# Attention scores on eight array tiles, attention sums on four, in pairs of PSUM banks, ahead of a gated feed-forward layer

## The chip, the cores and the metric

The kernel runs on one core of one Trainium2 chip. The metric is the device time of one execution in microseconds (us). A core has five engines that run side by side and meet only at semaphores: TensorE (PE, matrix products; its loads of stationary operands are listed apart as PEld), VectorE (DVE), ScalarE (ACT), GpSimd (POOL) and SyncE (SP, which issues the DMAs here). TensorE writes to PSUM, which has eight banks of 512 fp32 values in each of 128 partitions.

## The reference

The inputs are q, k, v of shape (4, 8, 768, 64), eight memory keys and values for each head, and the weights of the second layer.

```python
for c in range(24):                                  # chunks of 32 queries
    k_ctx = k[:, :, max(0, 32*c - 16) : min(768, 32*c + 40)]
    k_full = concatenate([mem_k, k_ctx], axis=2)     # up to 64 keys, v_full alike
    s = matmul(q_c, k_full.T) / 8
    a = exp(s - max(s)); a = a / (sum(a) + 1e-9)
    out[:, :, 32*c : 32*c + 32] = matmul(a, v_full)
x = heads put side by side                           # (4, 768, 512)
h = maximum(x @ w_in, 0)                             # (4, 768, 1024)
conv = 3-tap convolution of h along the sequence, a tap triple for each channel
result = (h / (1 + exp(-conv))) @ w_out              # (4, 768, 512)
```

The weights reach the chip as 64-bit floats. The kernel decodes each into a high and a low part.

## The kernel before, in words

**Attention.** There are 32 steps (`attention(n)`): four batches, two halves of the sequence, four pairs of heads. A step holds 12 chunks of two heads, that is 24 products of 32 queries by 64 keys. The host lays q, k and v out for it (`_laid_out`).

- *Scores* (L375 to L389). 24 fp32 matmuls, each with a stationary operand of 64 rows (the head's 64 dimensions) by 32 queries and 64 moving columns (keys). A row half of the array belongs to a head, and of the eight 64x32 tiles that the array has, four are used: head 0 writes to partition blocks 0 and 2, head 1 to blocks 1 and 3. TensorE runs an fp32 matmul as two passes, each with its own load of the stationary operand, so the trace has 48 matmul and 48 load records for a step. The scores fill 384 columns of one bank (pool `s`, two banks).
- *Softmax* (L391 to L439). DVE takes the maxima (L393); then DVE subtracts and ACT takes one exponential (L398, L404), or ACT takes six with a bias (L419). DVE sums (L431) and inverts (L433), and DVE or POOL multiplies (L436).
- *Turn* (L443 to L484). In a step of kind P, TensorE transposes three 128x128 blocks into a bank (L448), and ACT copies the result with two instructions (L455) into `a_d`. That tile is as wide as two row halves with zeros in half of it, so that a product over all 128 rows picks one chunk's keys for each half of the columns. In a step of kind B, DVE transposes 32x32 blocks (L466), and three DMAs take the result through DRAM. The string `TURN` names each step's kind: 15 P and 17 B.
- *Sums* (L486 to L497, `values`). 12 fp32 matmuls on two 128x64 tiles: 128 rows (two chunks of 64 keys), 64 columns of stationary v, 64 moving columns of `a_d`, so 24 passes. ACT (L498) and DVE (L501) take the result from its bank into a high and a low part. Turned blocks and sums share the pool `ta`, two banks.

**Feed-forward.** `ffn_in` is 768 matmuls of 384 columns (L517), with a ReLU on ACT; `gated` is the convolution, a tanh and products on DVE, ACT and POOL; `ffn_out` is 552 matmuls of 512 columns and 48 of 256 (L579). They use the other four banks (pool `f`).

**Order.** The list `ORDER` fixes the order in which all 1,545 operations are issued, and so the order on every engine. TensorE works strictly in it: between stretches of feed-forward matmuls stand short excursions to scores and sums. Strings of letters (`TAP`, `MULT`, `LO`, `SOFT`, `NORM`, `CLEAR`) choose the engine of an operation for each step or block. The costs in `plan.op` are not executed. A tile takes a free slot of its pool when its first operation is issued and gives it back after its last.

Of the kernel before, what the change touches and what calls it, by code (L numbers as in the profile page):

```python
# [22 lines left out]
KC = STEP * (NC - 1) + KW  # L23
# [6 lines left out]
W_IN, W_OUT, W_CONV = "RCMSMMCC", "MmCMCCmM", "r"  # L30
TAP = "AAAVAAAAVAAAAAAAVAAAVVAVVVVVVVAA"
MULT = "VVGVGGGGGVVVGVVVVVVVGVGVVVVVGVVG"
LO = "VVVGVVVVGVVGVGVGVVVGVVGGVVGVGGGG"
SOFT = "VVVVCCACVVCAVVVCVACACCCCCACCCCVV"
NORM = "VVGGGVGGGGVVVGGGVVGGGVGVGVVGGVVG"
CLEAR = "GAGAVAAGAGGVVAVAVVGAGGVGAAVVAVGV"
KEEP = "KKKNNNNKNKNKKNNKKKKNKNNNKKNNNKKN"
HOME = "wwwwwwwwwwxwwwwwxwwwwwwwxxwxxwxw"
TURN = "PPPPPPPPBPPBBPBPBPBBBBPBBBBPBBBB"

NU, NK, NE, NA, N64, ND = 40, 3, 3, 2, 4, 4

ORDER = [
# [154 lines left out]
def attention_then_gated_ffn(  # L198
# [35 lines left out]
    for x in slots("a_d", NA, [P, 2, 4 * NG, CH]):  # L234
        G.memset(x, 0.0)
# [127 lines left out]
    def attention(n):  # L363
# [79 lines left out]
        if TURN[n] == "P":  # L443
            t = Tile("ta")

            def turn():
                for g in range(NG):
                    nc.tensor.transpose(out=t.t[:, g * P : (g + 1) * P], in_=e.t[:, g, 1 : 2 * KW + 1], identity=ident)  # L448
# [255 lines left out]
```

## Time and profile before

| | |
|---|---|
| median of three runs | 350.18 us (350.15 to 351.26) |
| the profiled execution's own time | 349.44 us |
| its span (first to last instruction) | 347.7 us |
| TensorE busy | 333.2 us, 96% of the span |
| loads of stationary operands | 297.8 us, 86% |
| DVE, ACT, POOL busy | 244.3, 202.7, 86.0 us |
| bytes moved by DMA | 49.10 MB, 141 GB/s |

Busy time is the union of an engine's records. Ends of matmul records are modelled and the records overlap, so for TensorE the starts say more than the durations. In tables of windows, (x4) is the number of records that touch the window.

### The profile page before, as it was taken

To read this page: it belongs to the slowest core of one execution; us is meant where nothing else is said; L and a number is where in the kernel's file an instruction comes from. 1 tells how busy PE (TensorE), PEld (TensorE's weight loads), DVE (VectorE), ACT (ScalarE), POOL (GpSimd) and SP (SyncE) were. 2 spreads that over 40 slices of the span, in tenths; PEclk is the share of its full clock that TensorE was granted. 3 is DMA by queue.
4 is the path that set the end of the run, shared out by engine and by line. 5 is a ranking of instruction groups with operands and counts; after the bars stand their busy time and mean duration, and the time that the engine had idled before them with its cause. 6 is when DMAs were issued, how large, how long until landed. Compare 5 with 4: busy or idle time off the path is not lost.

```text
span 347.7 us, 8950 instructions
## 1 busy us (share of the span) xinstructions
PE 333.2 (96%) x3717; PEld 297.8 (86%) x3717; DVE 244.3 (70%) x406; ACT 202.7 (58%) x447; POOL 86.0 (25%) x83
## 2 busy tenths in 40 slices
PE   1599999999999999999999999999999999999996
PEld 1488999999999999899888889899998888888886
DVE  3999999999989999889999659611285698220000
ACT  3488969899888899366786385322426633320111
POOL 3324121165524103220002462020002395020000
PEclk9999999999999999999999999999999999999999
DMA  7998877757777435602244533311000001110202
GB/s 270 399 304 267 290 274 237 233 176 220 247 223 254 147 119 169 205 20 83 90 139 146 180 116 116 128 47 43 20 0 32 31 30 48 61 74 0 92 35 86
DMA packets 27256, 49.10 MB, mean 141 GB/s; under 512 B 3152, under 2 KB 18128, under 8 KB 27216
## 3 DMA queue, kind: packets, MB, share of 16 engines
q1 hardware_dynamic: 27216, 48.53, 42.1%
q8 instruction: 29, 0.48, 0.5%
q14 instruction: 11, 0.09, 0.1%
HBM read 38.89 MB, written 9.63 MB: 140 GB/s over the span
## 4 chain that ended last, share of the span: by engine, by line
PE 92%; DMA 3%; DVE 3%; ACT 1%; SPq 0%; POOL 0%; issue 0%; ACTq 0%
PE f L579 39%; PE f L517 38%; PE ta L495 8%; PE s L384 6%; DMA w<-in_w_in_dram 2%; PE ta L448 2%; DMA w<-in_v_dram 1%; DVE e L436 0%; DVE w_top L287 0%; SPq L262 0%; POOL w_out_lo L344 0%; DVE e L398 0%; DVE z L431 0%; DVE top L393 0%; DVE w_top L294 0%
## 5 line engine op out<-in xcount | busy, mean ns | idle before, releaser
L517 PE MATMUL f<-u,w_in_hi 128*128 128x384 f32 x512 | 141.8, 343 | 0.0
L579 PE MATMUL f<-w_out_hi,u 128*128 128x512 f32 (+1 forms) x400 | 125.9, 387 | 0.0
L517 PEld LDWEIGHTS f<-u,w_in_hi 128*128 128x128 f32 x512 | 93.5, 188 | 2.1
L579 PEld LDWEIGHTS f<-w_out_hi,u 128*128 128x128 f32 x400 | 74.1, 188 | 15.6
L517 PE MATMUL f<-u,w_in_lo 128*128 128x384 f32 x256 | 86.4, 337 | 0.0
L547 DVE SCALAR_TENSOR_TENSOR u<-u,cw,u 128x767 f32<-128x767 f32 x64 | 70.9, 1121 | 10.6 <-ACT u L538 9.5
L579 PE MATMUL f<-w_out_lo,u 128*128 128x512 f32 (+1 forms) x200 | 77.2, 386 | 0.0
L517 PEld LDWEIGHTS f<-u,w_in_lo 128*128 128x128 f32 x256 | 48.1, 188 | 0.8
L590 ACT COPY w_top<-f 128x512 f32<-128x512 f32 (+1 forms) x25 | 14.1, 569 | 54.9 <-PE f L579 47.3
L527 ACT ACTIVATE u<-f 128x384 f32<-128x384 f32 x64 | 30.4, 492 | 25.1 <-PE f L517 25.0
L579 PEld LDWEIGHTS f<-w_out_lo,u 128*128 128x128 f32 x200 | 37.6, 188 | 7.2
L567 POOL TENSOR_TENSOR u<-u,u 128x768 fp32r<-128x768 f32 x13 | 25.9, 2006 | 67.6 <-ACT u L564 46.3
L436 POOL TENSOR_TENSOR e<-e,z 128x384 f32<-128x384 f32 x18 | 15.6, 866 | 79.4 <-DVE z L433 60.1
L564 ACT CAST u<-u 128x768 fp32r<-128x768 f32 x32 | 26.1, 835 | 11.9 <-PE f L579 6.6
L551 ACT ACTIVATE u<-u 128x768 f32<-128x768 f32 x32 | 26.7, 846 | 8.9 <-DVE u L547 8.9
L561 POOL TENSOR_TENSOR u<-u,u 128x768 f32<-128x768 f32 x11 | 23.2, 2117 | 28.4 <-ACT u L560 28.4
L567 DVE TENSOR_TENSOR u<-u,u 128x768 fp32r<-128x768 f32 x19 | 21.8, 1160 | 10.8 <-ACT u L564 4.7
L501 DVE TENSOR_TENSOR u<-ta,u 128x384 fp32r<-128x384 f32 x32 | 17.1, 541 | 16.7 <-ACT u L498 16.3
L556 DVE SCALAR_TENSOR_TENSOR u<-u,u 128x768 f32<-128x768 f32 x21 | 21.7, 1034 | 9.9 <-ACT u L551 9.9
L419 ACT ACTIVATE e<-s,top 128x64 f32<-128x64 f32 x120 | 26.6, 327 | 3.2 <-DVE top L411 2.1
L498 ACT CAST u<-ta 128x384 fp32r<-128x384 f32 x32 | 15.0, 479 | 14.4 <-PE ta L495 14.3
L384 PE MATMUL s<-k,u 64*32 64x64 f32 x1344 | 23.4, 219 | 0.0
(59 smaller groups left out, 336.9 us busy)
## 6 DMA issues: line engine op xcount, KB each, us to landing
u<-in_v_dram SPq DMA_DIRECT2D x25, 384.0 KB, 5.0
k<-in_k_dram SPq DMA_DIRECT2D x28, 252.0 KB, 3.7
u<-in_q_dram SPq DMA_DIRECT2D x32, 192.0 KB, 4.1
out_dram<-w_top SPq DMA_DIRECT2D x23, 256.0 KB, 2.0
w<-in_w_in_dram SPq DMA_DIRECT2D x8, 512.0 KB, 5.5
w<-in_w_out_dram SPq DMA_DIRECT2D x8, 512.0 KB, 4.6
t_dram<-w SPq DMA_DIRECT2D x17, 192.0 KB, 2.3
a_d<-t_dram SPq DMA_DIRECT2D x34, 96.0 KB, 3.1
```

What stands on the lines that cost most here:

```text
L384: nc.tensor.matmul(s.t[j * D + h * CH : j * D + (h + 1) * CH, o : o + KW], lhsT=q_[r, c], rhs=k_t.t[r, c * STEP : c * STEP + KW], start=Tr ...
L419: A.activation(keys(e)[:, g // 2, g % 2], s_()[:, g // 2, g % 2], AF.Exp, bias=top.t[:, g : g + 1], scale=SCALE)
L495: nc.tensor.matmul(y, lhsT=v_g[:, g, u, h], rhs=a_d.t[:, :, o], start=True, stop=True)
L517: nc.tensor.matmul(f.t[:, :TW], lhsT=w_in_p[c][:, fc, cc], rhs=x.t[:, a * TW : (a + 1) * TW], start=(cc == 0 and i == 0), stop=(cc == NCC ...
L527: "A", act(TW, True), lambda: A.activation(h.t[:, hf * TW : (hf + 1) * TW], f.t[:, :TW], AF.Relu, scale=0.5), (f,), ((h, hf),)
L547: lambda j=j, to=to, at=at: V.scalar_tensor_tensor(out=c.t[:, to], in0=h.t[:, at], scalar=w[j], in1=c.t[:, to], op0=ALU.mult, op1=ALU.add) ...
L551: plan.op("A", act(S), lambda: A.activation(c.t, c.t, AF.Tanh), (c,), (c,), table="exp")
L556: lambda: V.scalar_tensor_tensor(out=y.t, in0=c.t, scalar=1.0, in1=h.t, op0=ALU.add, op1=ALU.mult),
L561: plan.op("G", 2.42 * S, lambda: G.tensor_tensor(out=y.t, in0=c.t, in1=h.t, op=ALU.mult), (c, h), (y,), shared=True)
L564: plan.op("A", act(S), lambda: A.copy(out=g_hi.t, in_=y.t), (y,), (g[0],))
L567: lambda: (V if lo == "V" else G).tensor_tensor(out=g_lo.t, in0=y.t, in1=g_hi.t.bitcast(F32), op=ALU.subtract),
L579: nc.tensor.matmul(ps.t[:, :n], lhsT=gs[b, fc][a].t[:, tt * P : (tt + 1) * P], rhs=w_out_p[c][:, fc, o : o + n], start=(fc == 0 and i == 0 ...
```

## The change

Half of a step's chunks now belong to each row half of the array. The row half u holds the six chunks of half u, for both heads, and the results of the two row halves go to two different banks of a pair. The scores use all eight 64x32 tiles: 24 matmuls of the same shape as before. The sums are 24 matmuls on four 64x64 tiles instead of 12 on two 128x64 tiles: 64 rows (one chunk's keys), 64 columns of stationary v, and 32 moving columns. `a_d` holds no zeros: it is half as wide, its memsets go, and in steps of kind P one ACT copy fills it. Scores, turned blocks and sums share one pool of two slots, each a pair of banks, where there were two pools of two banks; `a_d` has three slots instead of two. The DMAs of kind B move the same bytes in runs of half the length. The host's layouts follow; the keys of a step are 528 columns wide instead of 504.

The order list and the strings of letters are new: 1,528 operations, 21 steps of kind P and 11 of kind B.

```diff
-W_IN, W_OUT, W_CONV = "RCMSMMCC", "MmCMCCmM", "r"
-TAP = "AAAVAAAAVAAAAAAAVAAAVVAVVVVVVVAA"
-MULT = "VVGVGGGGGVVVGVVVVVVVGVGVVVVVGVVG"
-LO = "VVVGVVVVGVVGVGVGVVVGVVGGVVGVGGGG"
-SOFT = "VVVVCCACVVCAVVVCVACACCCCCACCCCVV"
-NORM = "VVGGGVGGGGVVVGGGVVGGGVGVGVVGGVVG"
-TURN = "PPPPPPPPBPPBBPBPBPBBBBPBBBBPBBBB"
+W_IN, W_OUT, W_CONV = "CCCmmCCM", "MCCCCCmM", "r"
+TAP = "AAAVAAAAVAAAAVAAAAAAVVVAAAAAVVAV"
+MULT = "VGGVGGGGGVVGGGVVGGGVGGVVGVVGVVGV"
+LO = "GVVVVVVVGVVVGGVVGVGVVVVGGVGGGVVV"
+SOFT = "ACVVVCCVVVCCVVVCCCVCVVCCCVACVAVC"
+NORM = "GVGGGGGGVGGGVGGVGGGGVVVVVVVGGGGG"
+TURN = "PPPPPPPPBPPPPPBPBPPPPPPPBBBBBBBB"
...
-    for x in slots("a_d", NA, [P, 2, 4 * NG, CH]):
-        G.memset(x, 0.0)
+    slots("a_d", NA, [P, TW])
...
-    slots("s", 2, [P, 512], pool=psum)
-    slots("ta", 2, [P, 512], pool=psum)
+    slots("s", 2, [P, 2, 512], pool=psum)
...
-                for p in range(2):
-                    for j in range(2):
-                        c = 4 * g + 2 * j + p
-                        o = (2 * g + p) * KW
-                        for h in range(2):
-                            r = slice(h * D, (h + 1) * D)
-                            nc.tensor.matmul(
-                                s.t[j * D + h * CH : j * D + (h + 1) * CH, o : o + KW],
-                                lhsT=q_[r, c], rhs=k_t.t[r, c * STEP : c * STEP + KW], start=True, stop=True,
-                            )
+                for j in range(4):
+                    c, h = 2 * g + j // 2, j % 2
+                    o = h * KH + c * STEP
+                    for u in range(2):
+                        r = slice(u * D, (u + 1) * D)
+                        nc.tensor.matmul(
+                            s.t[j * CH : (j + 1) * CH, u, g * KW : (g + 1) * KW],
+                            lhsT=q_[r, c, h], rhs=k_t.t[r, o : o + KW], start=True, stop=True,
+                        )
...
-            for p in range(2):
-                r = slice(p * D, (p + 1) * D)
-
-                def place(r=r, p=p):
-                    A.copy(
-                        out=a_d.t[r, p].rearrange("p (r g) q -> p g r q", g=NG),
-                        in_=t.t[r, : NG * P].rearrange("p (g r q) -> p g r q", r=4, q=CH),
-                    )
+            plan.op("A", act(TW, True), lambda: A.copy(out=a_d.t, in_=t.t[:, 0, :TW]), (t,), (a_d,))
...
-            v_g = v_().rearrange("p (g c h d) -> p g c h d", g=NG, c=2, h=2)
-            for g in range(NG):
-                for u in range(2):
-                    for h in range(2):
-                        r = slice(h * D, (h + 1) * D)
-                        if TURN[n] == "P":
-                            o, y = (2 * u + h) * NG + g, a.t[r, g * P + u * D : g * P + (u + 1) * D]
-                        else:
-                            o, y = h * 6 + 2 * g + u, a.t[r, g * P : (g + 1) * P].rearrange("p (j u q) -> p u j q", j=2, u=2)[:, u]
-                        nc.tensor.matmul(y, lhsT=v_g[:, g, u, h], rhs=a_d.t[:, :, o], start=True, stop=True)
+            v_c = v_().rearrange("p (c h d) -> p c h d", c=HC, h=2)
+            for c in range(HC):
+                g, p = c // 2, c % 2
+                for h in range(2):
+                    j = 2 * p + h
+                    o = (4 * g + j) * CH if TURN[n] == "P" else (NG * j + g) * CH
+                    for u in range(2):
+                        r = slice(u * D, (u + 1) * D)
+                        nc.tensor.matmul(
+                            a.t[h * D : (h + 1) * D, u, c * CH : (c + 1) * CH],
+                            lhsT=v_c[r, c, h], rhs=a_d.t[r, o : o + CH], start=True, stop=True,
+                        )
```

## Rows read from the trace of the kernel before

**Rows 1.** The page: busy time, share of the span and instructions of each engine.
```profile
PE 333.2 (96%) x3717; PEld 297.8 (86%) x3717; DVE 244.3 (70%) x406; ACT 202.7 (58%) x447; POOL 86.0 (25%) x83
```
**Rows 2.** The page: the chain that ended last, by engine.
```profile
PE 92%; DMA 3%; DVE 3%; ACT 1%; SPq 0%; POOL 0%; issue 0%; ACTq 0%
```
**Rows 3.** Windows of 20 us: length, busy us and records by engine, clock, DMA share, GB/s.
```profile
20.00:40.00 20.00, 20.00 (x392) 18.30 (x388) 19.80 (x46) 17.65 (x54) 4.39 (x5) 1.00 0.87 291
40.00:60.00 20.00, 20.00 (x331) 19.33 (x328) 19.04 (x44) 15.98 (x43) 5.54 (x10) 1.00 0.73 238
...
140.00:160.00 20.00, 20.00 (x274) 18.24 (x273) 16.81 (x27) 11.34 (x22) 4.47 (x4) 1.00 0.39 119
...
300.00:320.00 20.00, 20.00 (x87) 16.09 (x87) 2.87 (x2) 4.08 (x6) 1.85 (x1) 1.00 0.10 39
```
**Rows 4.** Waits of TensorE over the whole span: us in total, times, longest us.
```profile
PE s L384 <- DMA u<-in_q_dram: 5.7, 1, 5.7
PE ta L448 <- DVE e L436: 2.6, 2, 2.0
...
PE ta L495 <- DMA w<-in_v_dram: 0.3, 1, 0.3
```
**Rows 5.** Timeline of TensorE, two excursions: start us, us, operation, records.
```profile
173.41 0.40 PE L579 MATMUL f<-w_out_hi,u 128*128 128x512 f32 x1
173.74 1.54 PE L384 MATMUL s<-k,u 64*32 64x64 f32 x96
...
175.55 0.39 PE L579 MATMUL f<-w_out_lo,u 128*128 128x512 f32 x1
...
202.05 0.40 PE L579 MATMUL f<-w_out_hi,u 128*128 128x512 f32 x1
...
206.29 0.34 PE L517 MATMUL f<-u,w_in_lo 128*128 128x384 f32 x1
206.47 0.33 PE L517 MATMUL f<-u,w_in_hi 128*128 128x384 f32 x1
```
**Rows 6.** Windows of line L384 alone, from an excursion's first scores: matmuls, then loads.
```profile
39.87:39.88 0.01, 0.01 (x2) 0.01 (x2) 1.00 0.41 154
...
39.87:39.90 0.03, 0.03 (x4) 0.03 (x5) 1.00 0.80 307
...
39.87:39.98 0.11, 0.11 (x8) 0.11 (x12) 1.00 0.52 196
39.87:41.10 1.23, 1.23 (x88) 1.23 (x92) 1.00 0.24 86
```
**Rows 7.** Windows of line L495 alone, from an excursion's first sums.
```profile
38.32:38.37 0.05, 0.05 (x2) 0.05 (x2) 1.00 1.21 489
38.32:38.39 0.07, 0.07 (x2) 0.07 (x4) 1.00 1.47 466
38.32:38.44 0.12, 0.12 (x4) 0.12 (x6) 1.00 1.12 373
38.32:39.60 1.28, 1.28 (x43) 1.28 (x45) 1.00 0.98 374
```
**Rows 8.** Windows of line L517 alone, from the first matmul after an excursion.
```profile
29.04:29.15 0.11, 0.10 (x1) 0.10 (x1) 1.00 0.90 330
29.04:29.16 0.12, 0.11 (x1) 0.12 (x2) 1.00 0.83 302
```
**Rows 9.** Timeline of TensorE, one turn inside a stretch of feed-forward.
```profile
25.11 0.49 PE L448 MATMUL ta<-ident,e 128*128 128x128 f32 x3
...
25.61 0.34 PE L517 MATMUL f<-u,w_in_lo 128*128 128x384 f32 x1
```
**Rows 10.** Groups of instructions: records, busy us, mean ns of one, idle before.
```profile
L556 DVE SCALAR_TENSOR_TENSOR u<-u,u 128x768 f32<-128x768 f32 x21 | 21.7, 1034 | 9.9 <-ACT u L551 9.9
...
L501 DVE TENSOR_TENSOR u<-ta,u 128x384 fp32r<-128x384 f32 x32 | 17.1, 541 | 16.7 <-ACT u L498 16.3
L498 ACT CAST u<-ta 128x384 fp32r<-128x384 f32 x32 | 15.0, 479 | 14.4 <-PE ta L495 14.3
```

More of the change, by code (lines that the diff above doesn't have):

```diff
@@ L22 @@
 NG = NC // 4
-KC = STEP * (NC - 1) + KW
+HC = NC // 2
+KH = STEP * (HC - 1) + KW
+KC = 2 * KH
 TINY = 1.75 * 2.0**-15
 WC = 512
-W_IN, W_OUT, W_CONV = "RCMSMMCC", "MmCMCCmM", "r"
-TAP = "AAAVAAAAVAAAAAAAVAAAVVAVVVVVVVAA"
-MULT = "VVGVGGGGGVVVGVVVVVVVGVGVVVVVGVVG"
-LO = "VVVGVVVVGVVGVGVGVVVGVVGGVVGVGGGG"
-SOFT = "VVVVCCACVVCAVVVCVACACCCCCACCCCVV"
-NORM = "VVGGGVGGGGVVVGGGVVGGGVGVGVVGGVVG"
-CLEAR = "GAGAVAAGAGGVVAVAVVGAGGVGAAVVAVGV"
-KEEP = "KKKNNNNKNKNKKNNKKKKNKNNNKKNNNKKN"
-HOME = "wwwwwwwwwwxwwwwwxwwwwwwwxxwxxwxw"
-TURN = "PPPPPPPPBPPBBPBPBPBBBBPBBBBPBBBB"
-NU, NK, NE, NA, N64, ND = 40, 3, 3, 2, 4, 4
-ORDER = [
[69 rows of a table removed]
+W_IN, W_OUT, W_CONV = "CCCmmCCM", "MCCCCCmM", "r"
[4 more added lines that the diff above has]
+NORM = "GVGGGGGGVGGGVGGVGGGGVVVVVVVGGGGG"
+CLEAR = "VVGGAGGAGGAGVVAAVAAGGAAAGAVVAGVG"
+KEEP = "KKNKKKKNKNKKNKKNNKKNKKNNKNKKKNKK"
+HOME = "wwwwwwwwxwxwwwwwwwwxwxwwwxxxwwxw"
+TURN = "PPPPPPPPBPPPPPBPBPPPPPPPBBBBBBBB"
+NU, NK, NE, NA, N64, ND = 40, 3, 3, 3, 4, 4
+ORDER = [
[68 rows of a table added]
 ]
@@ L247, in attention_then_gated_ffn @@
     slots("z", 4, [P, 2 * NG])
-    slots("s", 2, [P, 512], pool=psum)
-    slots("ta", 2, [P, 512], pool=psum)
+    slots("s", 2, [P, 2, 512], pool=psum)
     slots("f", 4, [P, 512], pool=psum)
-    slots("t_dram", ND, [2, 2, CH, 2, NG * KW], pool=dram)
+    slots("t_dram", ND, [2, 4, CH, 2, NG * CH], pool=dram)
     w_in_p = [const.tile([P, NFC, NCC, P], F32R, name=f"w_in_{p}") for p in ("hi", "lo")]
@@ L375, in scores @@
         def scores():
-            q_ = q_d.t[:, :TW].rearrange("p (c q) -> p c q", q=CH)
+            q_ = q_d.t[:, :TW].rearrange("p (c h q) -> p c h q", c=HC, h=2)
             for g in range(NG):
-                for p in range(2):
-                    for j in range(2):
-                        c = 4 * g + 2 * j + p
-                        o = (2 * g + p) * KW
-                        for h in range(2):
-                            r = slice(h * D, (h + 1) * D)
-                            nc.tensor.matmul(
-                                s.t[j * D + h * CH : j * D + (h + 1) * CH, o : o + KW],
-                                lhsT=q_[r, c], rhs=k_t.t[r, c * STEP : c * STEP + KW], start=True, stop=True,
-                            )
-        plan.op("PE", 700, scores, (q_d, k_t), (s,), mode="tiled", late=250)
-        s_ = lambda: s.t[:, :W].rearrange("p (g u k) -> p g u k", u=2, k=KW)
+                for j in range(4):
[7 more added lines that the diff above has]
+                        )
+        plan.op("PE", 365, scores, (q_d, k_t), (s,), mode="t32", late=250)
+        s_ = lambda: s.t[:, :, : NG * KW].rearrange("p u (g k) -> p g u k", k=KW)
         plan.op(
@@ L439, in attention @@
         )
-        a, a_d = Tile("ta"), Tile("a_d")
+        a, a_d = Tile("s"), Tile("a_d")
         x = x_of[b, hf, cc] = Tile("u", dtype=F32R)
         if TURN[n] == "P":
-            t = Tile("ta")
+            t = Tile("s")
             def turn():
                 for g in range(NG):
-                    nc.tensor.transpose(out=t.t[:, g * P : (g + 1) * P], in_=e.t[:, g, 1 : 2 * KW + 1], identity=ident)
-            plan.op("PE", 327, turn, (e,), (t,), mode="whole", late=250)
-            for p in range(2):
-                r = slice(p * D, (p + 1) * D)
-                def place(r=r, p=p):
-                    A.copy(
-                        out=a_d.t[r, p].rearrange("p (r g) q -> p g r q", g=NG),
-                        in_=t.t[r, : NG * P].rearrange("p (g r q) -> p g r q", r=4, q=CH),
-                    )
-                plan.op("A", 480, place, (t,), ((a_d, p),), less=-20)
+                    nc.tensor.transpose(out=t.t[:, 0, g * P : (g + 1) * P], in_=e.t[:, g, 1 : 2 * KW + 1], identity=ident)
+            plan.op("PE", 245, turn, (e,), (t,), mode="whole", late=250)
+            plan.op("A", act(TW, True), lambda: A.copy(out=a_d.t, in_=t.t[:, 0, :TW]), (t,), (a_d,))
         else:
@@ L466, in attention @@
                 lambda: V.transpose(
-                    out=flat().rearrange("p (x g u q) -> p g u x q", x=2, g=NG, u=2),
+                    out=flat().rearrange("p (u x g q) -> p g u x q", u=2, x=2, g=NG),
                     in_=keys(e).rearrange("p g u (x k) -> p g u x k", x=2),
@@ L472, in attention, with place @@
                 "DMA", 530,
-                lambda: nc.sync.dma_start(out=d.t.rearrange("j h y x n -> (j h y) (x n)"), in_=flat()), (t,), (d,), gap=620,
-            )
-            for j in range(2):
-                def place(j=j):
+                lambda: nc.sync.dma_start(
+                    out=d.t.rearrange("u j y x n -> (j y) u (x n)"),
+                    in_=flat().rearrange("p (u n) -> p u n", u=2),
+                ), (t,), (d,), gap=620,
+            )
+            for u in range(2):
+                def place(u=u):
@@ L478, in place @@
                     nc.sync.dma_start(
-                        out=a_d.t[j * D : (j + 1) * D, j].rearrange("p (h o) q -> p h (o q)", h=2),
-                        in_=d.t[j].rearrange("h y x n -> (y x) h n"),
+                        out=a_d.t[u * D : (u + 1) * D].rearrange("p (j n) -> p j n", j=4),
+                        in_=d.t[u].rearrange("j y x n -> (y x) j n"),
                     )
-                plan.op("DMA", 350, place, (d,), ((a_d, j),), late=200, gap=650)
+                plan.op("DMA", 350, place, (d,), ((a_d, u),), late=200, gap=650)
@@ L497, in attention @@
-        plan.op("PE", 700, values, (v_t, (a_d, 0), (a_d, 1)), (a,), mode="tiled", late=250)
-        plan.op("A", act(TW, True), lambda: A.copy(out=x.t[:, :TW], in_=a.t[:, :TW]), (a,), ((x, 0),))
+            v_c = v_().rearrange("p (c h d) -> p c h d", c=HC, h=2)
[4 more added lines that the diff above has]
+                    o = (4 * g + j) * CH if TURN[n] == "P" else (NG * j + g) * CH
+                    for u in range(2):
+                        r = slice(u * D, (u + 1) * D)
[3 more added lines that the diff above has]
+                        )
@@ L499, in attention @@
+        plan.op("PE", 350, values, (v_t, (a_d, 0), (a_d, 1)), (a,), mode="t64", late=250)
+        a_ = lambda: a.t[:, :, : HC * CH]
+        halves = lambda y: y.rearrange("p (u n) -> p u n", u=2)
+        plan.op("A", act(TW, True), lambda: A.copy(out=halves(x.t[:, :TW]), in_=a_()), (a,), ((x, 0),))
         plan.op(
@@ L501, in attention @@
             lambda: V.tensor_tensor(
-                out=x.t[:, TW:S], in0=a.t[:, :TW], in1=x.t[:, :TW].bitcast(F32), op=ALU.subtract
+                out=halves(x.t[:, TW:S]), in0=a_(), in1=halves(x.t[:, :TW]).bitcast(F32), op=ALU.subtract
             ), (a, (x, 0)), ((x, 1),),
@@ L522, in ffn_in @@
             plan.op(
-                "PE", 520.5, mm, ((x, 0), (x, 1), (f"in{fc}", 0), (f"in{fc}", 1)), (f,),
+                "PE", 525, mm, ((x, 0), (x, 1), (f"in{fc}", 0), (f"in{fc}", 1)), (f,),
                 mode="whole", late=250,
@@ L584, in ffn_out @@
                 plan.op(
-                    "PE", 3 * n * 0.4535, mm, (*gs[b, fc], (f"out{fc}", 0), (f"out{fc}", 1)), (ps,),
+                    "PE", 3 * n * 0.455, mm, (*gs[b, fc], (f"out{fc}", 0), (f"out{fc}", 1)), (ps,),
                     mode="whole", late=250,
@@ L643, in windows @@
         return w
-    qt = q.reshape(B, H // 2, 2, NH, NC, CH, D).transpose(0, 3, 1, 2, 6, 4, 5)
-    ql = qt.reshape(B, NH, H // 2, 2 * D, NC * CH)
-    w = windows(k, mem_k).reshape(B, H // 2, 2, NH, NC, KW, D)
-    kl = np.empty((B, H // 2, 2, NH, KC, D), k.dtype)
-    for c in range(NC):
+    ql = q.reshape(B, H // 2, 2, NH, 2, HC, CH, D).transpose(0, 3, 1, 4, 7, 5, 2, 6).reshape(B, NH, H // 2, 2 * D, NC * CH)
+    w = windows(k, mem_k).reshape(B, H // 2, 2, NH, 2, HC, KW, D)
+    kl = np.empty((B, H // 2, 2, NH, 2, KH, D), k.dtype)
+    for c in range(HC):
         kl[..., c * STEP : c * STEP + KW, :] = w[..., c, :, :]
-    kl = kl.transpose(0, 3, 1, 2, 5, 4).reshape(B, NH, H // 2, 2 * D, KC)
-    w = windows(v, mem_v).reshape(B, H // 2, 2, NH, NG, 2, 2, KW, D)
-    vl = np.empty((B, NH, H // 2, 2 * KW, NG * 4 * D), v.dtype)
+    kl = kl.transpose(0, 3, 1, 4, 6, 2, 5).reshape(B, NH, H // 2, 2 * D, KC)
+    w = windows(v, mem_v).reshape(B, H // 2, 2, NH, 2, HC, KW, D)
+    vl = np.empty((B, NH, H // 2, 2 * KW, NC * D), v.dtype)
     for n, kind in enumerate(TURN):
@@ L658, in _laid_out @@
         if kind == "P":
-            y = y.transpose(3, 4, 1, 2, 0, 5)
+            y = y.transpose(1, 3, 2, 0, 4)
         else:
-            y = y.reshape(2, NG, 2, 2, 2, CH, D).transpose(2, 5, 4, 1, 3, 0, 6)
-        vl[b, hf, cc] = y.reshape(2 * KW, NG * 4 * D)
+            y = y.reshape(2, 2, HC, 2, CH, D).transpose(1, 4, 3, 2, 0, 5)
+        vl[b, hf, cc] = y.reshape(2 * KW, NC * D)
     return [np.ascontiguousarray(a) for a in (ql, kl, vl)]
```

137 rows, old and new, of the table ORDER are left out of this document.

## The prediction

> **What bounds the kernel now.** The page's shares come first: TensorE is busy for 96% of the span, DVE for 70% [rows 1]. The chain of waits says the same from the end: 92% of it is TensorE [rows 2]. Then the windows, which show where: from 20 us on TensorE has no idle time in any 20 us, at a granted clock of 1.00 (2.4 GHz), and DVE stands close beside it at first (19.8, 19.0 and still 16.8 us of 20), but hardly runs in the last 40 us [rows 3]. Last TensorE's own waits: they lie before the first feed-forward matmul at 21 us (queries, softmax), and afterwards 0.3 us is left [rows 4]. So the time is about 21 us of start plus the sum of what TensorE does, and a nanosecond taken from an attention step after the start counts in full, as long as DVE keeps up.
>
> The sum goes against the profiled execution's own 349.44 us (span 347.7 and 1.7 around it); the median shown is 0.74 above it.
>
> **Scores.** Four matmuls start within 30 ns, about 7 ns apart, then nothing starts until the array is free; in the steady part 80 matmuls take 1.12 us, so 56 ns for each four, one on each of four tiles, and a step's 48 passes take 12 x 56 = 0.67 us [rows 6]. The change puts eight passes in a round. Eight starts at 7 ns are 56 ns, just what a round takes. So 6 x 56 = 0.34 us, and 0.34 saved. Both new lists have five score steps before the first feed-forward matmul, where the waits of rows 4 set the time; I count nothing there. 27 x 0.336 = 9.1 us. The bounds: 0 if instructions can't come twice as densely (the densest sustained row is this one, 96 in 0.67 us), 9.1 if they can. I take 9.1, since the bursts at the head of rows 6 come at the denser rate.
>
> **Sums.** This is the term that decides. The steady part shows 39 passes in 1.16 us, 59 ns a pair, so 24 passes take 0.71 us [rows 7]. What sets the 59 ns, the 64 moving columns or the load of 64 stationary ones? At the head of an excursion the load has nothing to hide behind. A tile's next load starts at most 30 ns after its first where 32 columns are loaded (the fifth load of rows 6, by 39.90), 50 to 70 ns where there are 64 [rows 7], 110 to 120 where there are 128 [rows 8]: about 0.86 ns a column. Four tiles load at once, in 30 ns and not in four times that. So a tile needs some 55 ns for each new operand of 64 columns, and the sums already sit at this limit: 59 ns, 3 more than the scores' 56 with the same 64 moving columns. After the change a pass has half the moving columns, but there are 48 passes and 48 loads of 64 columns on four tiles: 12 loads in a row on each, as before. 12 x 59 = 0.71 us, nothing saved. The bounds: 12 x 28 = 0.34 us if the load halves with its rows, a gain of 0.36 in 31 steps (the 32nd lies in the start), 11.3 us; and 24 x 59 = 1.42 us if two row halves of one column strip load one after the other, a loss of 22.
>
> The Trainium skill speaks against this part (TensorE: Matmul & The Clock Gate, LDWEIGHTS (loading the stationary operand)): a load's time goes with its columns, and loading fewer rows saves nothing. That rows 6 to 8 agree on the columns is measured; that half the rows cost the same on a 64x64 tile no row here shows, and I lean on the page for it. By that rule the sums stay at 0.71 us; without it they could fall to 0.34. The skill also says (TensorEngine Tiling (Array Packing), Instruction Overhead) that a matmul of a few columns takes as long as one of 60, so that one shouldn't tile away an already small dimension; by that alone the pass would not shrink either.
>
> **Turns.** 21 steps turn on TensorE where 15 did; three transposes cost 25.11 to 25.61 less one matmul of 0.18, so 0.33 us [rows 9]. All six additions lie after the start: +2.0 us.
>
> **Excursions.** A change of tile shape costs TensorE time. A score-only excursion of two steps takes 173.41 to 175.55, less two matmuls of 20/86 = 0.232: 1.68, of which 1.34 is scores, so 0.33 is overhead [rows 3, 5]. One with four stretches takes 202.05 to 206.29, less 0.232, 0.18 and a turn of 0.33: 3.50, of which 1.34 and 1.42 are work, so 0.74 [rows 5]. That makes 0.20 for each excursion and 0.14 for each stretch. I counted the lists after the first feed-forward matmul: 20 excursions with 43 stretches before, 33 with 48 now. 13 x 0.20 + 5 x 0.14 = +3.3 us.
>
> **Edits at no cost.** ACT's second copy in a turn and POOL's memsets go; ACT and POOL are at 58% and 25% [rows 1], so nothing follows. The bounce through DRAM is made by 11 steps instead of 17, in shorter runs; feed-forward matmuls stand between a step's softmax and its sums, and without that cover a slower landing would stop TensorE as the 0.3 us of rows 4 did. Reads from pairs of banks have as many elements; I take 479 and 541 ns as they are [rows 10]. Should each such read cost a second start, DVE and ACT pay, not TensorE.
>
> **DVE.** The letters take some 11 us from it in all: products 21 to 14 (7 x 1.03 = 7.2), block transposes 17 to 11, and smaller ones [rows 10]. But I also counted the lists by these costs: where 40 us of TensorE work have been listed, 57 us of DVE work stood ahead of it before, 62 now; at 100 us, 124 and 126; at 160 it is less than before. DVE has 1.2 us to spare from 20 to 60 us [rows 3]. So it can hold TensorE up early, by 0 to 4 us; I take 1.5.
>
> **Sum.** 349.4 - 9.1 + 0 + 2.0 + 3.3 + 1.5 = 347.1 in the profiled execution, some 347.5 against the median; I say 347.4. Its own range, by DVE's 0 to 4 us and some tenths in each other term, is 344 to 351.
>
> **Rivals.**
> - *The sums halve too.* For it: 64 moving columns alone fill 56 of the 59 ns, as the scores' rounds show [rows 6], and half the columns would take 28. Against it: the load's 55 ns, and the 3 ns that the sums take more than the scores. TensorE's sum falls by a further 11.3 us, and then DVE, full to 160 us [rows 3], becomes the bound of the first half: by the count at 100 us of listed work it stands at 134 us instead of 124, which takes back 4 to 9. 347.4 - 11.3 + 5 = 341 (336 to 345).
> - *Two slots instead of four.* Scores, turns and sums all wait for the same two pairs of banks, and TensorE, in order, stops with every feed-forward matmul behind it. For it: after the start 76 uses pass through two slots, a sum's slot is held for ACT's 0.48 and then DVE's 0.54 us [rows 10], and DVE's queue is full. In the new list some twenty uses have under 1.8 us of TensorE work between them and the one whose slot they take. Against it: the rest have more. At 0.1 us for each use it costs 7.6 us; from 0.04 us a use on it eats the whole gain. Then 347.4 + 7.6 = 355, slower.
> - *The row halves don't load together.* For it: no row shows two loads in one column strip. Against it: a 128-row load does both halves in the same 50 to 70 ns [rows 7]. The sums cost 22 us more; the scores' two loads of 28 ns still fit in 56. 369 us.
> - *The scores don't do what the change says*, because the instructions come no denser than in rows 6: 347.4 + 9.1 = 356.
>
> **How the numbers follow.** I give my forecast 0.47, halved sums 0.26, the slots 0.12, serial loads 0.08, scores unchanged 0.07. The range from 336 to 355 holds the first, nearly all of the second and half of the third. A difference of 0.3%, 1.05 us, is about what can be told from none. Of my forecast's 0.47, 0.33 lies under 349.1 and 0.10 between that and 351.2; with the second rival 0.58 is faster. The slots give 0.02 to no change and the rest to slower, as the last two do: 0.58, 0.12, 0.30.
>
> **What would show it.** Scores: eight matmul starts in one round of 56 ns, 0.34 us a step. Sums: rounds of four every 59 ns, 0.71 us; rounds of 28 would show the load isn't the limit, of 118 that row halves take turns. Excursions: 0.20 and 0.14 us again. TensorE's waits: a new line on ACT or DVE for the pool `s` would be the slots; waits on DVE's softmax between 20 and 100 us would be DVE as the bound. The prediction fails if the sums' rounds are not near 59 ns, or if those waits exceed 4 us in all.

## The result, and the profile after

The changed kernel takes 353.94 us (median; 353.34 to 354.82) where the kernel before took 350.16 beside it: a ratio of 1.0108, 95% interval 1.0072 to 1.0143. It is 1.1% slower. The forecast was 347.4 us, so it had the wrong sign; the time lies inside the wide range (336 to 355) and outside the likeliest case's own (344 to 351). The profiled execution took 354.14 us, span 352.0. Of all the executions told of below, one was in a slower state (356.28 us, of the kernel before with surplus matmuls), and its time is left out.

The page's busy times, which answer to [rows 1], and its chain by engine, which answers to [rows 2]:

```profile
PE 337.0 (96%) x4503; PEld 297.0 (84%) x4503; DVE 225.9 (64%) x387; ACT 205.0 (58%) x436; POOL 96.0 (27%) x91
...
PE 93%; DVE 4%; DMA 1%; issue 1%; ACT 1%; DVEq 0%; ACTq 0%
```

TensorE still sets the time, and now has 786 more matmuls and as many more loads. The same windows as in [rows 3], up to 160 us:

```profile
20.00:40.00 20.00, 19.14 (x388) 16.67 (x386) 14.26 (x33) 9.74 (x30) 6.80 (x7) 1.00 0.71 244
40.00:60.00 20.00, 20.00 (x426) 18.53 (x423) 18.45 (x43) 14.98 (x40) 5.82 (x13) 1.00 0.86 290
140.00:160.00 20.00, 20.00 (x403) 17.95 (x385) 14.95 (x32) 15.53 (x38) 7.16 (x6) 1.00 0.33 108
```

In the first window DVE does 14.3 us where it did 19.8, and ACT 9.7 instead of 17.7. So DVE is not what holds TensorE up there; it has room. TensorE's waits over the whole span, as in [rows 4]:

```profile
PE s L383 <- DMA u<-in_k_dram: 5.7, 1, 5.7
PE s L383 <- DMA u<-in_q_dram: 2.7, 2, 1.8
PE s L447 <- ACT a_d L450: 1.0, 1, 1.0
PE s L383 <- ACT e L418: 0.9, 1, 0.9
PE s L487 <- issue: 0.9, 1, 0.9
PE s L447 <- DVE u L498: 0.4, 1, 0.4
```

All of these lie before 23.1 us; the same view from 31.3 us on is empty. One is new in kind: 0.9 us ("issue") in which the sums waited for nothing that the view shows. The last of the experiments shows what that was: their own instructions.

**The start.** TensorE's timeline (start us, us, operation, records, idle before):

```profile
19.41 0.67 PE L514 MATMUL f<-u,w_in_hi 128*128 128x384 f32 x1
...
20.65 1.49 PE L487 MATMUL s<-a_d,u 64*64 64x32 f32 x45
23.00 0.42 PE L487 MATMUL s<-a_d,u 64*64 64x32 f32 x3 [0.86 <-issue]
...
27.44 0.52 PE L514 MATMUL f<-u,w_in_lo 128*128 128x384 f32 x1
27.76 0.84 PE L514 MATMUL f<-u,w_in_hi 128*128 128x384 f32 x2
28.40 0.52 PE L514 MATMUL f<-u,w_in_lo 128*128 128x384 f32 x1
...
31.34 0.42 PE L514 MATMUL f<-u,w_in_hi 128*128 128x384 f32 x1
31.60 0.34 PE L514 MATMUL f<-u,w_in_lo 128*128 128x384 f32 x1
31.78 0.34 PE L514 MATMUL f<-u,w_in_hi 128*128 128x384 f32 x1
```

Feed-forward begins 1.8 us earlier than before (19.41 against 21.18). But from there to 31.2 us a matmul of 384 columns takes 0.32 us from start to start (27.44, 27.76, then two by 28.40), and from 31.60 on 0.175. That is 1.2 columns a nanosecond and then 2.2: the lower of the clock's two levels (1.2 GHz) and then the higher (2.4 GHz), although the clock column of the first window says 1.00. Before the change the higher level began at 20.45 us. Both starts are those of one execution each; how far they vary is told with the experiments.

**Scores.** Windows of line L383 alone, from an excursion's first scores (as [rows 6]):

```profile
32.04:32.12 0.08, 0.07 (x8) 0.07 (x15) 1.00 1.11 454
32.04:32.18 0.14, 0.13 (x16) 0.13 (x24) 1.00 1.12 461
...
32.04:32.29 0.25, 0.24 (x32) 0.24 (x33) 1.00 1.22 500
32.04:32.46 0.42, 0.41 (x40) 0.41 (x43) 1.00 1.07 434
32.04:32.60 0.56, 0.55 (x48) 0.55 (x48) 1.00 1.03 407
```

The rounds of eight matmuls in 56 ns are there (8 by 32.12, 16 by 32.18). They last for 32 passes, that is 32 loads and 32 matmuls. The next eight take 0.17 us by these windows, the last eight 0.14: from the start of the 32nd to that of the 48th it is 0.27 us, 17 ns a pass. A step is not done in 0.34 us.

Two excursions on TensorE's timeline, for [rows 5]: two steps of scores, and one of sums with one of scores.

```profile
52.52 0.34 PE L514 MATMUL f<-u,w_in_hi 128*128 128x384 f32 x1
52.78 1.24 PE L383 MATMUL s<-k,u 64*32 64x64 f32 x96
53.95 0.45 PE L514 MATMUL f<-u,w_in_hi 128*128 128x384 f32 x1
54.24 0.33 PE L514 MATMUL f<-u,w_in_lo 128*128 128x384 f32 x1
...
207.96 0.90 PE L487 MATMUL s<-a_d,w 64*64 64x32 f32 x48
208.79 0.72 PE L383 MATMUL s<-k,u 64*32 64x64 f32 x48
```

From 52.52 to 54.24, less two matmuls of 0.175, is 1.37 us, where it was 1.67. With the same 0.34 of overhead two steps cost 1.03, one 0.52; single-step excursions say the same (0.851 − 0.34 = 0.51; 1.006 before). So a step saves some 0.15 us, where 0.34 was forecast.

**Sums.** Windows of line L487 alone (as [rows 7]):

```profile
39.12:39.15 0.03, 0.03 (x4) 0.03 (x4) 1.00 0.92 273
...
39.12:39.27 0.15, 0.15 (x10) 0.15 (x12) 1.00 0.44 137
39.12:39.82 0.70, 0.70 (x48) 0.70 (x48) 1.00 0.72 269
```

Four loads and four matmuls start within the first 0.03 us, then rounds of four follow every 58 ns: a step of 48 passes takes 0.70 us, as the 24 passes did before.

### The profile page after: what moved, and what is told of

The parts are those of the page before. It is cut to its first block, busy times and chain, and to the rows that moved or that the text cites. A ratio compares the mean times of both kernels' runs of the same rounds, so it can differ in the third digit from the quotient of the medians.

```text
span 352.0 us, 10491 instructions
## 1 busy us (share of the span) xinstructions
PE 337.0 (96%) x4503; PEld 297.0 (84%) x4503; DVE 225.9 (64%) x387; ACT 205.0 (58%) x436; POOL 96.0 (27%) x91
## 4 chain that ended last, share of the span: by engine, by line
PE 93%; DVE 4%; DMA 1%; issue 1%; ACT 1%; DVEq 0%; ACTq 0%
PE f L514 40%; PE f L576 38%; PE s L487 8%; PE s L383 5%; PE s L447 2%; DMA w<-in_w_in_dram 1%; DVE top L392 1%; DVE e L435 1%; DVE w_top L294 0%; DVE w L307 0%; DVE w_top L281 0%; DVE z L430 0%; DVE e L397 0%; DVE u L498 0%; ACT u L495 0%
## 5 line engine op out<-in xcount | busy, mean ns | idle before, releaser
L514 PE MATMUL f<-u,w_in_hi 128*128 128x384 f32 x512 | 148.1, 350 | 0.0
L514 PEld LDWEIGHTS f<-u,w_in_hi 128*128 128x128 f32 x512 | 95.3, 191 | 2.9 <-issue 0.2
L558 POOL TENSOR_TENSOR u<-u,u 128x768 f32<-128x768 f32 x18 | 36.0, 2005 | 55.6 <-ACT u L557 43.0
L524 ACT ACTIVATE u<-f 128x384 f32<-128x384 f32 x64 | 30.9, 499 | 29.5 <-PE f L514 29.1
L435 POOL TENSOR_TENSOR e<-e,z 128x384 f32<-128x384 f32 x21 | 20.8, 988 | 69.6 <-DVE z L432 57.0
L498 DVE TENSOR_TENSOR u<-s,u 128x384 fp32r<-128x384 f32 x32 | 17.6, 554 | 22.9 <-ACT u L495 22.4
L495 ACT CAST u<-s 128x384 fp32r<-128x384 f32 x32 | 15.4, 481 | 26.1 <-PE s L487 23.6
L564 POOL TENSOR_TENSOR u<-u,u 128x768 fp32r<-128x768 f32 x11 | 20.6, 1884 | 29.1 <-ACT u L561 16.7
L487 PEld LDWEIGHTS s<-a_d,u 64*64 64x64 f32 x1152 | 20.6, 145 | 5.8 <-issue 2.4
L553 DVE SCALAR_TENSOR_TENSOR u<-u,u 128x768 f32<-128x768 f32 x14 | 14.0, 997 | 16.6 <-ACT u L548 16.6
L487 PE MATMUL s<-a_d,u 64*64 64x32 f32 x1152 | 22.9, 229 | 1.0 <-issue 0.9
```

What stands on the lines that cost most here:

```text
L435: lambda: (V if norm == "V" else G).tensor_tensor(out=keys(e), in0=keys(e), in1=pairs(z.t).unsqueeze(3).broadcast_to([P, NG, 2, KW]), op=A ...
L487: nc.tensor.matmul(a.t[h * D : (h + 1) * D, u, c * CH : (c + 1) * CH], lhsT=v_c[r, c, h], rhs=a_d.t[r, o : o + CH], start=True, stop=True,)
L498: lambda: V.tensor_tensor(out=halves(x.t[:, TW:S]), in0=a_(), in1=halves(x.t[:, :TW]).bitcast(F32), op=ALU.subtract), (a, (x, 0)), ((x, 1),),
L514: nc.tensor.matmul(f.t[:, :TW], lhsT=w_in_p[c][:, fc, cc], rhs=x.t[:, a * TW : (a + 1) * TW], start=(cc == 0 and i == 0), stop=(cc == NCC ...
L524: "A", act(TW, True), lambda: A.activation(h.t[:, hf * TW : (hf + 1) * TW], f.t[:, :TW], AF.Relu, scale=0.5), (f,), ((h, hf),)
L558: plan.op("G", 2.42 * S, lambda: G.tensor_tensor(out=y.t, in0=c.t, in1=h.t, op=ALU.mult), (c, h), (y,), shared=True)
```

## The experiments

**Scores on four tiles in turn.** The program gives TensorE all of one row half, then the other.

```diff
-            for g in range(NG):
-                for j in range(4):
-                    ...
-                    for u in range(2):
+            for u in range(2):
+                for g in range(NG):
+                    for j in range(4):
```

> The changed kernel with the loop over row halves put outermost in the scores, so that four tiles work at a time. Theory A (eight tiles help the scores until TensorE's queue of ready instructions is empty, and a step now takes 0.52 us instead of 0.67): a score step goes back to 12 rounds of 56 ns, 0.67 us, and the kernel is 27 x 0.15 = 4.0 us slower than the changed one, about 358. Theory B (instructions alone set the scores' time, eight tiles bring nothing): no change, 354. Theory C (the eight tiles bring the full 0.34 us of the forecast and the loss lies elsewhere): 9 us slower, 363.

355.79 us (354.65 to 356.15), ratio 1.016 (1.0128 to 1.0193). The single-step excursion is 899 ns, so 0.56 us a step; from 32 us to the end it loses 1.5 us against the changed kernel. The first theory had 4 us, from rounds of four. But TensorE did not keep to four tiles. Windows of its scores, from an excursion's first:

```profile
44.84:44.97 0.13, 0.13 (x8) 0.13 (x12) 1.00 1.07 130
44.84:45.06 0.22, 0.22 (x20) 0.22 (x28) 1.00 0.70 86
44.84:45.17 0.33, 0.33 (x33) 0.33 (x35) 1.00 0.67 128
```

Between 0.13 and 0.22 us twelve matmuls start, where four tiles start four in 56 ns [rows 6]: the second row half already works beside the first, ahead of the program's order. So this run does not set four tiles against eight, and it neither bears out nor refutes the 4 us. What eight tiles are worth is read against the kernel before: 0.67 us a step there, 0.52 here.

**Sums with 64 moving columns.** Each matmul of the sums gets the double width, as long as the next column block exists; results of the surplus columns are overwritten.

```diff
+                        w = min(2 * CH, TW - o)
...
-                            lhsT=v_c[r, c, h], rhs=a_d.t[r, o : o + CH], start=True, stop=True,
+                            lhsT=v_c[r, c, h], rhs=a_d.t[r, o : o + w], start=True, stop=True,
```

> The changed kernel with 64 moving columns in each sum instead of 32 (the surplus is overwritten by the next chunk's sum). Theory A (the load of 64 stationary columns sets the round of 58 ns): rounds stay at 58 to 60 ns, the time at 354 within 1. Theory B (moving columns and a fixed cost set it): rounds grow by 27 ns, 12 x 27 ns x 31 steps = 10 us slower, 364.

353.85 us (351.98 to 355.72), ratio 1.0111 (1.0065 to 1.0157). Two steps of sums cost 1745 ns beside 1732, still in rounds of 58 ns. Doubling the moving columns costs nothing in the steady part, so they don't set the round; with the 50 to 70 ns of a load of 64 columns [rows 7], the load does. The head of an excursion fits: the second round starts 107 ns after the first with 64 moving columns and 79 with 32, since there the load has nothing to hide behind. A run that loads fewer columns on these tiles was not made.

**TensorE busy from the start, three ways.** Surplus matmuls on the identity go into a bank of feed-forward that is not yet in use: 27 of 128 columns in the changed kernel, 26 in the kernel before, then eight of 512 in the changed kernel (each run has one of the three lists).

```diff
-        for i in ORDER:
+        for at, i in enumerate(ORDER):
+            self.warm(WARM.get(at, 0))
...
+WARM = {15: 10, 26: 6, 36: 3, 46: 3, 67: 3, 90: 1, 102: 1}   # 27 of 128 columns
+WARM = {16: 10, 30: 8, 46: 6, 67: 2}                          # 26, kernel before
+WARM = {15: 3, 26: 2, 36: 1, 46: 1, 67: 1}                    # 8 of 512 columns
```

> The changed kernel with 27 surplus fp32 matmuls of 128x128 by 128 columns on the identity, put between TensorE's first operations, where it waits. Theory A (TensorE runs at the lower of its two clocks until 31 us, since it was too little busy before; in the kernel before only until 20): the feed-forward matmuls from 19 to 31 us come every 0.175 us instead of 0.32, sums and scores there at twice the rate; 12 x 0.145 + 3 x 0.6 = 3.5 us faster, 350.5. Theory B (the late start comes from waits for data and instructions, and the clock costs nothing): 354 or slower by the surplus matmuls.

356.92 us (354.73 to 358.38), ratio 1.0193 (1.0139 to 1.0247): slower still. Its largest wait of TensorE:

```profile
PE s L387 <- issue: 4.3, 3, 2.4
```

Of these, 2.4 us end at 15.3 us and 1.6 at 54.4, and the higher clock began for good only at 25.5 us.

> The kernel before with 26 such surplus matmuls. There the clock is up at 20.5 us, before the first feed-forward matmul. Theory A: only the latency of a few early steps shrinks, 0 to 1.5 us faster, 349 to 350. Theory B (surplus matmuls stand in the way): 1 to 2 us slower.

351.75 us (350.99 to 353.61), ratio 1.0044 (1.001 to 1.0078). The kernel before loses too, with 1.4 us of such a wait at 22 us. Surplus matmuls bring instructions of their own into the stretch where these come late.

> The changed kernel with eight surplus fp32 matmuls of 128x128 by 512 columns between TensorE's first operations: as long a work as in e3, with 32 records instead of 108. Theory A (e3 lost its gain to waits for instructions: those of TensorE arrive in blocks of 16 KB, and the DMA engines are full until 24 us): no idle time put down to issue over 1 us before 20 us, the clock up from 5 us and high at 23 to 31 us, 2 to 3.5 us faster than the changed kernel, 351. Theory B (surplus work at the start delays the chain whatever its instructions): as e3, 355 to 357.

353.07 us (352.58 to 354.03), ratio 1.0099 (1.0073 to 1.0124): 0.9 us less than the changed kernel, but the ranges overlap, so the times don't tell the two apart. The higher clock holds from some 4.5 us on. At the 21st feed-forward matmul TensorE is 3.2 us ahead of the changed kernel (28.57 against 31.78 us), at the 151st 1.0 (65.19 against 66.20). In between stand two waits of TensorE, at 33.4 and 49.2 us:

```profile
PE s L387 <- issue: 1.0, 1, 1.0
...
PE s L491 <- issue: 0.5, 1, 0.5
```

Both are for instructions. Its waits on POOL, ACT and DVE lie before 28.6 us. So in this execution an early clock is worth one microsecond at the end and not three, and most of the rest went to instructions that came late, not to the engines that feed TensorE.

The start of the higher clock also differs where nothing was done to it. With the changed kernel's order and no surplus matmuls the higher level began at 31.2 us in the profile after, but at some 28 us in the run with 64 moving columns, whose TensorE was 1.0 us ahead at the 21st feed-forward matmul and still at the 151st. The first feed-forward matmul started between 19.4 and 20.8 us in these traces.

**The kernel before, its excursions split.** Order alone: 33 excursions and 43 stretches of one shape, as many excursions as the changed kernel has, where there were 20 with as many stretches. The kind of edit (S a step's scores, V its sums):

```diff
-S V S V  feed-forward
+S V  feed-forward  S V  feed-forward
```

> The kernel before with nothing changed but the order list: 13 excursions are cut in two by the next feed-forward group, so that there are 33 with 43 stretches, instead of 20 with 43. Theory A (each excursion costs 0.20 us beside its stretches): 13 x 0.20 = 2.6 us slower, 352.9. Theory B (only a change of shape between stretches costs, and those were counted right): 0.14 us less for each stretch that the cut saves, none here: 350.3.

354.81 us (353.66 to 355.37), ratio 1.0134 (1.0103 to 1.0165). The excursions' own cost rises by 2.5 us in the trace, 0.19 for each of the 13. That is the term of the forecast. The rest of the loss, some 2.3 us, lies in waits and in the first 25 us, and no run isolates it.

**Two thirds of the scores.**

```diff
-            for g in range(NG):
+            for g in range(NG if n < 5 or n == 7 else 2):
```

> The changed kernel with only 16 of a step's 24 score matmuls, after the first six steps; the last third of the scores keeps what the bank held, so the output is not the reference's. Theory A (TensorE has 64 instructions, 32 passes, ready when an excursion starts, and more come at 16 to 17 ns a pass): the 32 passes run in four rounds of 56 ns, and a single step takes 0.26 us less than now (0.59 for an excursion with one score step, where it is 0.85). Theory B (every pass costs the same 10.9 ns): a third of 0.52, 0.17 less (0.68).

One time, 351.31 us; the kernel leaves out the last third of the scores in all steps but six. An excursion with one step of scores falls from 851 to 582 ns: the 16 passes left out cost 0.27 us, 17 ns each, where the rounds of 56 ns would have given 0.11. The first theory gave 0.26, the second 0.17. Two steps in a row then tell whether the slow passes are a matter of their count or of their place in the step. Windows of that stretch alone:

```profile
52.21:52.49 0.28, 0.27 (x33) 1.00 1.04 366
52.21:52.64 0.43, 0.42 (x41) 1.00 1.01 360
52.21:52.87 0.66, 0.65 (x64) 1.00 1.02 372
```

The first 32 passes again run in rounds of 56 ns. The 33rd now is the first of the second step, with the columns that ran fast in the first, and the eight from there on take 0.15 us. So it is not the place in the step. Nor is it the time since the excursion's start: with the row halves in turn, above, it takes 0.32 us to the 33rd pass and not 0.27, and the slow passes begin there too. In the changed kernel at the lower clock it takes 0.43:

```profile
26.05:26.48 0.43, 0.43 (x33) 0.43 (x33) 1.00 0.14 50
26.05:26.69 0.64, 0.64 (x46) 0.64 (x48) 1.00 0.13 48
```

So the count decides. The Trainium skill (Advanced Engine Details and Errata, Engine Queue Depths) gives TensorE's queue 64 entries: 32 loads and 32 matmuls, which is where the rounds end here. That the passes then wait for instructions is argued, not shown, and as a fixed rate of instructions it does not fit: 17 ns a pass is slower than the 14 that [rows 6] keep up over 80 passes, and at the lower clock the first 32 passes leave time for 25 more at 17 ns and still end at 32. What is shown is the pace: 16 to 17 ns in single-step excursions, at either clock (13 passes in 0.21 us in the rows above), and 64 passes in 0.76 us, 11.8 ns each, after the first 32 of a two-step excursion, where rounds of eight need 7.

**Three input loads issued later** (order alone, changed kernel): the loads of three steps' queries that stood ahead of the late sums go behind them, from 20.8 us to 29.1 us.

```diff
-load  load  load  ...  sums  ...  feed-forward block
+sums  ...  load  load  load  feed-forward block
```

> The changed kernel with the loads of three steps' queries (0.6 MB), which are used after 45 us, issued some 10 us later than now (at 20 to 23 us). Theory A (TensorE's wait of 0.86 us at 22 us is for a block of instructions behind full DMA engines): the wait falls under 0.3 us and the three feed-forward matmuls after it come earlier by as much. Theory B (it waits for a semaphore that the trace doesn't show): the wait stays.

One time, 354.8 us. The wait for instructions at the sums falls from 0.86 to 0.24 us, and the higher clock still begins only at 31.7 us. But the sums go on no earlier, at 23.28 us and not 23.00, and so do the three feed-forward matmuls behind them: the wait is shorter because TensorE itself came 0.9 us later. So the first theory is not borne out.

**Equal shapes put together in the kernel before.** Order inside excursions alone: 32 stretches instead of 43.

```diff
-S V S V
+S S V V
```

> The kernel before, with TensorE's order changed inside its excursions alone, so that operations of one tile shape stand together: still 20 excursions after the first feed-forward matmul, 32 stretches of equal shape where there were 43. Theory A (a change of shape costs 0.14 us wherever it stands, and nothing else decides): 11 x 0.14 = 1.5 us faster than the kernel before, about 348.6, with two-step scores at 1.34 us and excursions costing 0.20 + 0.14 for each stretch as before. Theory B (what a stretch saves is taken back by waits, since the moved scores or sums hold a slot longer or start before DVE or ACT has delivered): 350.2 or slower, with new waits of TensorE's lines for scores and sums on DVE or ACT.

350.48 us (349.11 to 351.46, 12 runs) beside 350.59, ratio 0.9988 (0.997 to 1.0006): no difference that can be told. One excursion, before and then in this kernel:

```profile
84.57 0.34 PE L517 MATMUL f<-u,w_in_hi 128*128 128x384 f32 x1
84.84 0.88 PE L384 MATMUL s<-k,u 64*32 64x64 f32 x48
85.64 0.92 PE L495 MATMUL ta<-a_d,u 128*64 128x64 f32 x24
86.49 0.88 PE L384 MATMUL s<-k,u 64*32 64x64 f32 x48
87.30 0.92 PE L495 MATMUL ta<-a_d,u 128*64 128x64 f32 x24
88.14 0.45 PE L517 MATMUL f<-u,w_in_hi 128*128 128x384 f32 x1
```

```profile
85.89 0.34 PE L526 MATMUL f<-u,w_in_hi 128*128 128x384 f32 x1
86.16 0.88 PE L393 MATMUL s<-k,u 64*32 64x64 f32 x48
87.25 0.88 PE L393 MATMUL s<-k,u 64*32 64x64 f32 x48 [0.22 <-DVE e L407]
88.06 1.62 PE L504 MATMUL ta<-a_d,u 128*64 128x64 f32 x48
89.61 0.45 PE L526 MATMUL f<-u,w_in_hi 128*128 128x384 f32 x1
...
91.22 0.44 PE L526 MATMUL f<-u,w_in_hi 128*128 128x384 f32 x1 [0.30 <-ACT u L536]
```

Undisturbed excursions of this form fall from 3505 to 3224 ns: 0.14 for each of two stretches, and over all 11 it is 1.5 us. But the second scores now come before DVE has emptied a slot of the pool, this excursion takes 3651, and ACT is late at 91.2. Such waits take 0.4 us back here, 0.6 in the excursion at 203 us and 0.7 between feed-forward matmuls. Both theories hold: the price is right, and waits take it back. The first feed-forward matmul starts at 22.20 us here and at 22.14 in the split kernel, against 21.18 in the profile before, though all three have the same order up to the excursion at 26 us: the start varies by 1 us from one execution to the next, and the one profiled before was an early one.

**Both edits of the start together**, in the changed kernel:

```diff
+WARM = {15: 3, 26: 2, 36: 1, 46: 1, 67: 1}                    # 8 of 512 columns
-load  load  load  ...  sums  ...  feed-forward block
+sums  ...  load  load  load  feed-forward block
```

> The changed kernel with both edits of the start together: the eight surplus matmuls of 512 columns that keep TensorE busy early, and the three groups of input loads issued later. Alone, the first gave 353.07 us, with 1.0 us of waits for instructions at the head of its scores and 1.7 at a feed-forward matmul's load, and the second took 0.6 us of such a wait away. Theory A (blocks of instructions stand behind the input loads, and these waits are what eats the head start of 3.2 us): the waits for instructions fall under 1 us in all, and the time falls to 351.5 to 352.5. Theory B (the head start is eaten by ACT, DVE and POOL, which work at their own pace until 60 us): the waits for instructions fall, others grow, and the time stays at 353.0 to 353.7, where the first edit alone had put it.

353.58 us (351.95 to 355.22), ratio 1.0082 (1.0053 to 1.0111). The waits for instructions did not fall:

```profile
PE s L396 <- issue: 1.2, 1, 1.2
...
PE s L500 <- issue: 0.8, 2, 0.6
```

The median is the second theory's, but its premise is missed as well. The profiled execution was the fastest of the eight (351.95 us) and kept a lead of 2.1 us over the changed kernel's from the 151st feed-forward matmul to the end; the median shows no such lead. No version here can be told to be faster than the kernel before.

What these waits are the traces do show. In all of them together TensorE waits 19 times for instructions, for 0.2 to 2.4 us. Each wait begins after 449 of its records (loads, matmuls and its own semaphore instructions) or after a multiple of 256 more, and each ends 1.2 to 1.6 us after a packet of 16 KB has landed on the instruction queue: in the changed kernel the packet lands at 21.44 us and the sums go on at 23.00, with the later loads at 21.92 and 23.28. So TensorE waits for the next packet, of 256 instructions, and surplus matmuls bring the ends of packets forward. What sets when a packet is sent is not shown.

## Why the prediction was wrong

The forecast's sum for the profiled execution was 347.1 us; it took 354.1. Of the 7.0 us two terms missed 5.1 and about 2.5, and some tenths came back in small ones: the 0.3 us wait of [rows 4] is gone, and a step of sums is a few ns shorter. (Against the median the sum is 347.8 by its own 0.74, not the 347.5 that the prediction writes; nothing hangs on it.)

- **Scores: the step that failed.** The prediction took the upper bound, 9.1 us, "since the bursts at the head of rows 6 come at the denser rate". Measured: 27 times some 0.15 us, 4.0. The miss is 5.1 us. The rows of before could not show a sustained rate above theirs (96 instructions in 0.67 us), and a burst shows only itself. The shortened scores show how far it goes: 32 passes, that is 64 instructions, of a step's 48 passes; the rest come at 17 ns each in single-step excursions. Why they do is not shown. With 4.0 in its place the same sum is 352.2, slower than before.
- **The start: undersized.** The prediction took 1.5 us for DVE holding TensorE up. Between 19.41 and 31.60 us TensorE does 19 feed-forward matmuls, a step of sums, one of sums with one of scores, and a turn. At what these cost later (0.175 each, 1.03, 1.69 and 0.33) that is 6.4 us; it takes 12.2. Of the 5.8 lost, 3.8 lie in the excursions (0.9 of it the wait for instructions) and 2.0 between feed-forward matmuls, at the lower clock. Less the 1.8 won before the first feed-forward matmul it is about 4.0. It was the wrong cause too: DVE has room there (14.3 us of 20). How much of it is the clock is not settled: with an early clock the medians are 0.9 and 0.4 us lower, at ranges that overlap, and the traces 1.0 and 2.2. Why the higher clock begins so late is not settled either. Up to 20 us TensorE is as busy as before (2.80 and 4.47 us in 10 to 15 and 15 to 20 us, 3.04 and 4.33 before the change); the gap of 0.86 at 22.1 us is new, but with later loads it is 0.24 and the clock is no earlier.
- **Sums: right.** 12 loads in a row on each tile at 58 ns, 0.70 us, nothing saved. The Trainium skill's rule on loads (TensorE: Matmul & The Clock Gate, LDWEIGHTS (loading the stationary operand)), on which half the rows cost the same, is borne out, and the run with 64 moving columns shows that the moving columns don't set the round. With that the rival of halved sums (341 us) falls, and so does that of row halves which load in turn (369).
- **Turns and excursions: right.** The 18 turns alone in feed-forward cost 0.33 us in the median. One step of sums costs 1033 ns alone, two steps 1732, sums with scores 1686: 0.20 for an excursion and 0.14 for a stretch fit them all. Both were then measured by themselves, 0.19 in the split order and 0.14 in the grouped one.
- **Two slots instead of four: wrong as a wait, half right elsewhere.** After 31.3 us one use waits for its slot beyond the usual 0.25 us of a change of shape: at 80.5 us the loads of sums stand 0.43 us, for DVE's read of scores (L397). So the 0.1 us a use was not there. Before the first feed-forward matmul three waits on readers of a slot are (1.0 and 0.9 us on ACT, 0.4 on DVE's L498), and that matmul still came earlier than before. But with two slots no excursion of the new order has more than two attention operations, where the old ones had up to four. That may be why there are 33 excursions, 3.3 us; no run gave the changed kernel more slots, so this stays an argument.
- **Scores unchanged (356 us)**, at a chance of 0.07, said that passes come no denser than in [rows 6]. From the 33rd pass on that holds in single-step excursions, whatever the reason; for the first 32 it does not.
- **Edits at no cost: right.** DVE's reads of a pair of banks take 554 ns beside 541, ACT's 481 beside 479 [rows 10]; POOL and ACT have room.

The working error behind the sign was to take one end of the scores' bounds, to give the other a chance of 0.07, and to leave out what lies between. Neither of the two signs by which the prediction said it would fail came, rounds of sums off 59 ns or waits over 4 us; what failed was the first thing that it said would be seen, a step of scores in 0.34 us.

## What to carry to other kernels

When tiles in turn would need instructions to come more densely than any long row of the trace shows, give the densest long row and the burst as the two bounds, and look for how long a burst lasts before taking its end: here 32 of 48 passes, and 4.0 us of 9.1. Splitting a product over row halves doubles the instructions; here it did not pay in the sums, where loads of 64 columns set the round, and it paid in part in the scores, where 64 moving columns did. A stretch of one tile shape has a price of its own, and an order that avoids it pays only as far as the engines that deliver to it keep up.

## What the runs showed of the hardware

- After feed-forward, 32 passes of small matmuls (32 loads and 32 matmuls) start 7 ns apart, eight to a round of 56 ns; from the 33rd on they average 11.8 ns over 64, with stretches of 16 to 17. At the lower clock the rounds of eight take 107 ns, and the pace from the 33rd pass on stays 16 to 17.
- On four 64x64 tiles a round of four loads and matmuls takes 58 ns with 32 and with 64 moving columns alike.
- Two loads in one column strip, on different row halves, do not take turns: four tiles' loads fit in the same 58 ns.
- TensorE's instructions arrive by a DMA queue of their own, in packets of 16 KB (35 packets, 0.57 MB; 29 packets before), and all 19 waits for instructions lie at the ends of stretches of 256. In the changed kernel a packet takes 0.9 to 1.3 us to land, and no longer where the 16 DMA engines are full (shares of 1.04 to 1.05 from 10 to 25 us); after a wait TensorE goes on 1.2 to 1.6 us after the landing. Waits lie where the engines are full and also where they are not (a share of 0.65 in the 3 us up to 43 us, with two thirds of the scores).
- On two row halves TensorE starts matmuls of the second ahead of some of the first that stand before them in the program (20 starts by 0.22 us, with the row halves in turn).
- The clock column of a window can read 1.00 while matmuls run at half rate; the distance between starts is the safer reading.
